# Reordering the two kinds of step in a convolution and soft-mixture kernel: the order of an odd and an even step's parts

## The chip, the cores and the metric

The kernel runs on one core of a Trainium2 chip. The time is device time in microseconds (us) of one execution, from several executions of the same program; the median is quoted. One execution was also taken by the hardware profiler, and everything said of the inside of the kernel comes from that one.

Names used below: PE is TensorE (matrix products and transposes, results in PSUM banks), DVE is VectorE, ACT is ScalarE, POOL is GpSimd, SP is the sync engine, whose queue here issues nearly all transfers (DMAs). Each engine and the SP queue work through their own instructions strictly in the order of the program; they wait for each other by semaphores.

## The reference: what is computed

Two parts, one after the other, in float32:

```python
# x: (8, 5696, 128), h: (5696, 128)
Xf = np.fft.rfft(x, n=2*S, axis=1); Hf = np.fft.rfft(h, n=2*S, axis=0)
y  = np.fft.irfft(Xf * Hf[None], n=2*S, axis=1)[:, :S]     # long convolution
x  = y.reshape(45568, 128)
logits = x @ phi                                           # phi: (128, 32)
d = softmax of logits over the 45568 tokens                # column-wise
slot_in = d.T @ x                                          # 32 slots x 128
slot_out = relu(slot_in[e] @ w1[e]) @ w2[e]                # 8 experts, 4 slots each
c = softmax of logits over the 32 slots                    # row-wise
out = c @ slot_out                                         # (45568, 128)
```

## The kernel before: tiles, stages and the order of the work

The convolution is done as a two-level transform. A sequence of 5696 rows is seen as 89 by 64; the first level works along the 89, the second along the 64, and then the same way back. Between levels the data change their layout by going through DRAM: tensor `f` between the first and the second level, tensor `z` between the second level and the way back. The filter `h` goes through the first two levels as batch 0, the eight batches of `x` follow.

The main loop (line 583) runs over steps t = 0, 1, 2 ... 92. Nine batches of 8 chunks make 72 chunks, and step t < 72 takes chunk t. The pieces of work, each named by one letter in the dictionary `work_` (lines 607 to 628):

- `x`, `load_x` (L184, L195): two SP transfers, 320 KB and 36 KB, of chunk t+3 into one of three tiles `xc`.
- `f`, `fold` (L201, L206): two POOL additions (sum and difference of the chunk with its mirror image) of chunk t+1 into `xf`, four tiles, two for even and two for odd chunks.
- `X`, `first_low` (L217, L220, L226): first-level products of chunk t for 60 of the 90 frequencies, in 128x64 shape; two ACT evictions, two SP stores to `f` of 240 KB.
- `Y`, `first_high`: the remaining 30 frequencies of chunks t-1 and t together, on odd t only, in 128x32 shape; two evictions, four stores of 120 KB. It is the last reader of chunk t-1's folded tiles, which `f` of the same step overwrites.
- `p`, `P`, `prefetch` (L253): SP loads of second-level units `gt` from `f` (512 KB each, the last of a batch 128 KB). A batch has 12 units; odd steps work on one, even steps on two.
- `b`, `slot_b`: for a unit u, `stage_b1` (PE L267 in 64x64 shape, then four DVE instructions, L285 twice and L294 twice), and `stage_b2` of the unit before it (PE L309, also 64x64; two ACT evictions L315; one 512 KB store to `z`, L318).
- `z`, `load_pair` (L338, L346): SP loads of one pair of output columns from `z`: five transfers (1024 KB, three of 128 KB, 32 KB) into `zc`, of which there is one tile only.
- `1`, `stage_c1` (L365, L370, L371, L374, L378): the way back. Two products of `zc` (call them c1a), an eviction and two DVE additions; then the function `between`, which is `stage_c4` of an older pair (PE transposes L431, ACT, DVE L446, POOL L439 and L447); then two more products (c1b) and an eviction.
- `w`: the rest of `stage_c1`, two DVE additions and four POOL ones (L384).
- `2`, `stage_c2` (L393): sixteen transposes of the result, four evictions L395. `3`, `stage_c3` (L402): products with phi, the logits, evicted to `lt` by L405. `m`, `column_max` (L413 and on): running column maximum of `lt` on DVE. `5`, `stage_c5` (L454). `s`, `softmax` (L462 to L468). `6`, `stage_c6` (L504, store L515). `d`, `dispatch` (L480, L485): accumulation of `d.T @ x`.

Products of PE go through a ring of four PSUM banks; each new result waits until the one four before it has been read. The order of the letters is written out by hand, one string for odd and one for even t:

```python
ORDER_E, ORDER_O, XAHEAD = "xXYf1wb5s", "zPxXfb26db3m", 3
for c_ in (ORDER_E if t % 2 else ORDER_O):
    work_[c_]()
```

`ORDER_E` is used on odd t, `ORDER_O` on even t. An odd step and the even step after it are called a pair of steps here; a pair handles one `zc`. Pairs of the way back begin at t = 27 (lag `LAG_C`), second-level units at t = 9. The last chunk is t = 71, so from then on `x`, `X`, `Y` and `f` do nothing. After the loop comes a tail written out separately (lines 658 to 851) with the last pairs, the experts and the output.

Of the kernel before, what the change touches and what calls it, by code (L numbers as in the profile page):

```python
# [12 lines left out]
AL = mybir.AluOpType  # L13
# [64 lines left out]
def kernel(  # L78
# [24 lines left out]
    nc = tc.nc  # L103
# [3 lines left out]
    E, _, F = moe_w1.shape  # L107
# [12 lines left out]
    NQ = NJ // 2  # L120
# [57 lines left out]
    xs = {}  # L178
# [17 lines left out]
                out=t_[X0 + r.start:X0 + r.stop, :, :, :].rearrange("p s n d -> p s (n d)"), in_=v)  # L196
        xs[c] = t_

    folded = {}

    def fold(c, comp):  # L201
        if c not in xs:
            return
        t_ = xs.pop(c) if comp else xs[c]
        y_ = xf[c % 2 * 2 + comp]
        nc.gpsimd.tensor_tensor(out=y_[:, :, :], in0=t_[:, 0, :, :], in1=t_[:, 1, ::-1, :],  # L206
                                op=AL.subtract if comp else AL.add)
        folded[(c, comp)] = y_

    def first_stage(tiles, width):  # L210

        st = apool.tile([P, CH, 2, D], F32, name="fst", tag="fst", bufs=4)
        for G in range(2):
            p = bank()
            for o, (c, comp) in enumerate(tiles):
                k = slice(0, HP) if width == HP else slice(HP, HP + QP)
                nc.tensor.matmul(p[o * width:(o + 1) * width, :], s1[:, comp + G, k],  # L217
                                 folded[(c, comp)][:, :, :].rearrange("p n d -> p (n d)"),
                                 start=True, stop=True)
            nc.scalar.activation(st[:, :, G, :],  # L220
                                 p[:, :].rearrange("p (n d) -> p n d", d=D), AF.Copy)
        for o, (c, comp) in enumerate(tiles):
            g, j = divmod(c, NJ)
            n0 = comp * HALF + CH * j
            k0, n = (0, N1A) if width == HP else (N1A, N1 - N1A)
            nc.sync.dma_start(  # L226
                out=fd[g].rearrange("q a r c d -> (q a) (r c d)")[k0:k0 + n, n0 * 2 * D:(n0 + CH) * 2 * D],
                in_=st[o * width:o * width + n, :, :, :].rearrange("k n c d -> k (n c d)"))
# [2 lines left out]
        first_stage([(c, comp) for comp in range(2)], HP)  # L231

    def first_high(c):

        both = [(c - 1 + i, comp) for i in range(2) for comp in range(2)]
        first_stage(both, QP)
        for b_ in both:
            del folded[b_]

    gs, prods = {}, {}  # L240

# [107 lines left out]
                                    a=2)[r:r + n, j * w_:(j + 1) * w_])  # L349
        zs[T] = t_  # L350

    def stage_c1(T, between):
        t_ = zs.pop(T)
        kr = used if t_ is zn else P
        y_ = ybufs.pop(0)
        ybufs.append(y_)

        def part(v, f):
            k = (2 * v + f) * CH
            return y_[:, k:k + CH, 0:D] if f == 0 else y_[:, k + CH - 1:k - 1:-1, 0:D]  # L360

        def product(o, tab, q):
            p = bank()
            for h_ in range(2):
                nc.tensor.matmul(p[h_ * HP:(h_ + 1) * HP, :], i1[0:kr, tab, :],  # L365
                                 t_[0:kr, h_, o, :, q, :], start=True, stop=True)
            return p[:, :].rearrange("p (n d) -> p n d", d=D)

        def fold_out(even, minus, plus):
            nc.vector.tensor_tensor(out=plus, in0=even, in1=minus, op=AL.add)  # L370
            nc.vector.tensor_tensor(out=minus, in0=even, in1=minus, op=AL.subtract)  # L371

        b_, a_ = product(0, 1, 1), product(0, 0, 0)
        nc.scalar.activation(part(0, 0), b_, AF.Copy)  # L374
        fold_out(a_, part(0, 0), part(1, 0))
        between()
        b_, a_ = product(1, 1, 0), product(1, 2, 1)
        nc.scalar.activation(om[:, :, :], b_, AF.Copy)  # L378

        def after():  # L380
            fold_out(a_, om[:, :, :], op[:, :, :])
            for v, o_, eng in ((1, op, nc.gpsimd), (0, om, nc.vector if tail else nc.gpsimd)):
                for part_, sign in ((part(v, 1), AL.subtract), (part(v, 0), AL.add)):
                    eng.tensor_tensor(out=part_, in0=part(v, 0), in1=o_[:, :, :], op=sign)  # L384

        ys[T] = y_
        return after

    def stage_c2(T):
        for k in (3, 1, 0, 2) if tail else (3, 2, 1, 0):  # L390
# [187 lines left out]
    for comp in range(2):  # L578
        fold(0, comp)
    wait_b2 = []  # L580
    ORDER_E, ORDER_O, XAHEAD = "xXYf1wb5s", "zPxXfb26db3m", 3

    for t in range(last_front + 1):
        us = list(units(t))

        def pair(lag):
            T, half = divmod(t - LAG_C - lag, 2)
            return T if half == 0 and 0 <= T < NT else None

        def prefetch(last):  # L590
            nonlocal loaded
            while loaded < len(queue) and queue[loaded][1] <= last:
                load_g(queue[loaded][0])
                loaded += 1

        def slot_b():
            fresh = bool(us)
            if fresh:
                u = us.pop(0)
                stage_b1(u, t < LAG_C or t >= NA)  # L600
                wait_b2.append(u)
            if len(wait_b2) > fresh:
                stage_b2(wait_b2.pop(0))

        T, U = pair(0), pair(2)
        after = []
        work_ = {
            "z": lambda: load_pair(pair(-1)) if pair(-1) is not None else None,
            "x": lambda: load_x(t + XAHEAD) if t < NA else None,
            "p": lambda: prefetch(t + 1) if t % NJ else None,  # L610
            "P": lambda: prefetch(t + 2),
            "q": lambda: prefetch(t + 1),
            "X": lambda: first_low(t) if t < NA else None,
            "Y": lambda: first_high(t) if t < NA and t % 2 else None,
            "f": lambda: [fold(t + 1, comp) for comp in range(2)] if t < NA else None,
            "d": lambda: dispatch(pair(3)) if pair(3) is not None else None,
            "b": lambda: slot_b(),
            "1": lambda: after.append(stage_c1(T, lambda: stage_c4(U) if U is not None else None))
            if T is not None else stage_c4(U) if U is not None else None,
            "w": lambda: [a_() for a_ in after],  # L620
            "2": lambda: stage_c2(pair(1)) if pair(1) is not None else None,
            "6": lambda: stage_c6(pair(5)) if pair(5) is not None else None,
            "5": lambda: stage_c5(U) if U is not None else None,
            "3": lambda: stage_c3(pair(1)) if pair(1) is not None else None,
            "m": lambda: column_max(pair(1)) if pair(1) is not None else None,
            "s": lambda: list(softmax(U)) if U is not None else None,
            "g": lambda: prefetch(t + 1) if t % NJ == 0 else None,
        }
        if t == last_front:
            if pair(-1) is not None:  # L630
                load_pair(pair(-1))
            assert T is None and U is None
            if pair(3) is not None:
                dispatch(pair(3))
            slot_b()
            slot_b()
            slot_b()
            stage_c2(pair(1))
            slot_b()
            assert not us and not wait_b2  # L640
            V = pair(1)
            stage_c6(V - 2)
            stage_c3(V)
            column_max(V)
            break
        for c_ in (ORDER_E if t % 2 else ORDER_O):
            work_[c_]()
        assert not us
        if t == NA:
            lead.close()  # L650
            wts = inner.enter_context(tc.tile_pool(name="wts", bufs=1, side="right"))
            w1s = wts.tile([P, E, F], F32, name="w1s")
        if NA < t <= NA + E:
            nc.sync.dma_start(out=w1s[:, t - NA - 1, :], in_=moe_w1[t - NA - 1])
# [21 lines left out]
    tail["pool"] = cload.enter_context(tc.tile_pool(name="cload", bufs=2))  # L676
    y_ = tail["pool"].tile([P, Q * CH, D + 1], F32, name="y2", tag="y2", bufs=1)

    after = stage_c1(T, lambda: stage_c4(V))
    after()  # L680
    stage_c5(V)
    list(softmax(V))
    nc.gpsimd.memset(y_[:, :, D:D + 1], 1.0)
# [21 lines left out]
    for V in range(T, NT):  # L705
# [10 lines left out]
        N = T + 1 if V == T else V + 2  # L716
        after = None
        if N < NT:
            after = stage_c1(N, lambda: stage_c4(V))
            load_pair(N + 2)  # L720
        else:
            stage_c4(V)
        if after:
            after()
        if V > T:
            placed_c()
        stage_c5(V)
# [8 lines left out]
            list(end)  # L736
        if V == T:
            ybufs.insert(0, y_)
            stage_c1(T + 2, lambda: None)()
            load_pair(T + 4)  # L740
        else:
            for i in range(4 * (V - T - 1), min(4 * (V - T), E), 2):
                nc.sync.dma_start(
                    out=w2s[:, i:i + 2, :, :],
                    in_=moe_w2[i:i + 2].rearrange("e (p c) d -> p e c d", p=P))
    stage_c6(NT - 2)
    assert list(Ls) == [NT - 1] and not (ys or ds or prods or gs or zs or xs or folded or wait_b2
                or kept or landed)


# [129 lines left out]
```

## Time and profile before

| what | value |
|---|---|
| median of 3 runs | 869.77 us (869.0 to 874.97) |
| the profiled execution: its own time | 869.39 us |
| its span, first to last instruction | 867.6 us |
| granted TensorE clock, mean | 0.947 |
| PE busy | 774.3 us (89%) |
| DVE busy | 619.5 us (71%) |
| ACT busy | 442.6 us (51%) |
| POOL busy | 404.3 us (47%) |
| transfers | 272.46 MB, mean 314 GB/s, 90.2% of the 16 DMA engines' span on SP's queue |

The shares are averages over stages of a different kind. In time the stages are, by the trace: up to about 53 us the first level alone (chunks of `h` and the first of `x`); to about 99 us second-level units of `h`; to 177 us second-level units of `x` as well; from the first c1a at 176.96 us to 627.33 us the full pairs, 22 of them; to about 720 us pairs without first-level work; then the tail.

### The profile page before, as it was taken

The numbers are of one execution on the slowest core, as the hardware profiler recorded it, in microseconds if no ns is written. First come the engines' busy times: TensorE is split into PE (matmuls) and PEld (weight loads), VectorE is DVE, ScalarE is ACT, GpSimd is POOL, SyncE is SP. The second block draws the span as 40 slices with busy tenths as digits, with TensorE's granted clock in tenths as the row PEclk, the third lists the DMA queues.
The fourth block names the chain that finished last, engine by engine and source line by source line (L and its number), as shares of the span: only waits on it lengthen the run. The fifth ranks groups of instructions, "written<-read, shape, count | busy, mean of one in ns | idle before, by whom it ended". The sixth has DMA issues, their size and how long they took to land.

```text
span 867.6 us, 20501 instructions
## 1 busy us (share of the span) xinstructions
PE 774.3 (89%) x7796; PEld 380.7 (44%) x7796; DVE 619.5 (71%) x929; ACT 442.6 (51%) x906; POOL 404.3 (47%) x386
## 2 busy tenths in 40 slices
PE   5889788889999999999999999999998888968993
PEld 1223333234444444444444444444454444444882
DVE  3049867667778778877888788777788895963642
ACT  2433244435555555655565565555544444773541
POOL 4453424245565566656566555555434332671000
PEclk9999999999999999999999999999999898988855
DMA  9899999999999999999999999999997886670898
GB/s 294 258 300 316 299 326 351 324 327 332 341 326 342 334 329 334 337 330 338 339 348 337 335 328 338 337 326 335 316 330 276 286 308 252 245 305 2 338 405 337
DMA packets 156124, 272.46 MB, mean 314 GB/s; under 512 B 12198, under 2 KB 113702, under 8 KB 152885
## 3 DMA queue, kind: packets, MB, share of 16 engines
q1 hardware_dynamic: 155451, 270.85, 90.2%
q8 instruction: 62, 1.02, 0.5%
q10 hardware_dynamic: 576, 0.31, 0.1%
q14 instruction: 35, 0.29, 0.1%
HBM read 142.81 MB, written 128.21 MB: 312 GB/s over the span
## 4 chain that ended last, share of the span: by engine, by line
PE 55%; DMA 20%; DVE 11%; SPq 2%; issue 2%; POOL 1%; ACT 1%; DVEq 0%; ACTq 0%
PE bank L365 13%; PE bank L217 11%; DMA zc<-z 8%; PE bank L309 7%; PE bt L267 7%; PE bank L393 6%; DMA out_dram<-o 4%; DMA xc<-in_x_dram 4%; DMA gt<-f 3%; DVE yf L294 3%; PE bank L480 3%; DVE p L285 2%; DVE bt L285 2%; SPq L346 2%; PE bank L431 2%
## 5 line engine op out<-in xcount | busy, mean ns | idle before, releaser
L206 POOL TENSOR_TENSOR x<-xc 128x512 f32<-128x512 f32 x144 | 180.1, 1275 | 228.5 <-PE bank L217 196.4
L217 PE MATMUL bank<-x,s 128*32 128x512 f32 (+1 forms) x1152 | 227.4, 613 | 16.3 <-POOL x L206 15.4
L315 ACT ACTIVATE zst<-bank 128x512 f32<-128x512 f32 (+1 forms) x184 | 98.7, 586 | 190.5 <-PE bank L309 168.8
L220 ACT ACTIVATE fst<-bank 128x512 f32<-128x512 f32 x216 | 127.5, 598 | 109.5 <-PE bank L217 85.0
L285 DVE TENSOR_TENSOR p<-bt,Hi 128x1024 f32<-128x1024 f32 x96 | 111.3, 1160 | 34.0 <-PE bt L267 33.1
L365 PE MATMUL bank<-zc,i 128*64 128x512 f32 x480 | 117.5, 611 | 10.8 <-DMA f<-fst 6.4
L309 PE MATMUL bank<-yf,vt 64*64 64x256 f32 x1440 | 102.4, 390 | 26.8 <-DVE yf L294 26.8
L217 PEld LDWEIGHTS bank<-x,s 128*32 128x32 f32 (+1 forms) x1152 | 57.0, 124 | 154.3 <-issue 76.1
L294 DVE TENSOR_TENSOR yf<-bt,p 128x512 f32<-128x512 f32 x192 | 119.3, 662 | 3.3
L267 PE MATMUL bt<-gt,wt 64*64 64x256 f32 x1620 | 113.7, 388 | 6.0 <-DMA gt<-f 3.9
L285 DVE TENSOR_TENSOR bt<-bt,Hr 128x1024 f32<-128x1024 f32 x96 | 112.9, 1177 | 0.0
L267 PEld LDWEIGHTS bt<-gt,wt 64*64 64x64 f32 x1620 | 54.0, 132 | 80.9 <-issue 38.0
L384 POOL TENSOR_TENSOR y<-y,op 128x512 f32<-128x512 f32 x64 | 77.5, 1211 | 11.4 <-DVE op L370 8.3
L309 PEld LDWEIGHTS bank<-yf,vt 64*64 64x64 f32 x1440 | 57.0, 135 | 58.0 <-issue 27.8
L370 DVE TENSOR_TENSOR y<-bank,y 128x512 f32<-128x512 f32 x32 | 22.1, 691 | 70.9 <-PE bank L365 70.6
L393 PE MATMUL bank<-ident,y 109*128 109x109 f32 x512 | 66.1, 283 | 0.7 <-DVE y L384 0.7
L384 POOL TENSOR_TENSOR y<-y,om 128x512 f32<-128x512 f32 x54 | 64.1, 1186 | 2.1
L365 PEld LDWEIGHTS bank<-zc,i 128*64 128x64 f32 x480 | 31.2, 137 | 74.6 <-issue 45.9
L393 PEld LDWEIGHTS bank<-ident,y 109*128 109x128 f32 x512 | 55.9, 154 | 16.5 <-issue 11.1
L395 ACT ACTIVATE yt<-bank 128x360 f32<-128x360 f32 x128 | 51.7, 489 | 4.2 <-PE bank L393 4.2
L833 PE MATMUL op<-so,cT 32*128 32x128 f32 x704 | 45.8, 378 | 3.6 <-ACT o L842 2.9
L285 DVE TENSOR_TENSOR p<-bt,turn 128x1024 f32<-128x1024 f32 (+1 forms) x12 | 14.2, 1179 | 46.6 <-PE bt L267 45.7
(97 smaller groups left out, 817.3 us busy)
## 6 DMA issues: line engine op xcount, KB each, us to landing
gt<-f SPq DMA_DIRECT2D x99, 512.0 KB
z<-zst SPq DMA_DIRECT2D x88, 512.0 KB
f<-fst SPq DMA_DIRECT2D x144, 240.0 KB
zc<-z SPq DMA_DIRECT2D x30, 1024.0 KB
xc<-in_x_dram SPq DMA_DIRECT2D x64, 320.0 KB
f<-fst SPq DMA_DIRECT2D x144, 120.0 KB
out_dram<-o SPq DMA_DIRECT2D x16, 1024.0 KB
zc<-z SPq DMA_DIRECT2D x90, 128.0 KB
```

The source lines that it names most:

```text
L206: nc.gpsimd.tensor_tensor(out=y_[:, :, :], in0=t_[:, 0, :, :], in1=t_[:, 1, ::-1, :], op=AL.subtract if comp else AL.add)
L217: nc.tensor.matmul(p[o * width:(o + 1) * width, :], s1[:, comp + G, k], folded[(c, comp)][:, :, :].rearrange("p n d -> p (n d)"), start=Tr ...
L220: nc.scalar.activation(st[:, :, G, :], p[:, :].rearrange("p (n d) -> p n d", d=D), AF.Copy)
L267: nc.tensor.matmul(bt[q * HP:(q + 1) * HP, a, o, :], wt[r, 2 * i + q, :], t_[r, 2 * o + q, :, :].rearrange("p c d -> p (c d)"), start=True ...
L285: nc.vector.tensor_tensor(out=p_, in0=pv, in1=h_, op=AL.mult)
L294: eng.tensor_tensor(out=y_[r, 0:k, c, :], in0=pv[:, :, c, :], in1=pi[r, 0:k, 1 - c, :], op=op_)
L309: nc.tensor.matmul(bz[q][a * HP:(a + 1) * HP, o * 2 * D:(o + 1) * 2 * D], vt[r, i, a, :], y_[r, a * m + o, :, :].rearrange("p c d -> p (c ...
L315: nc.scalar.activation(st[:, 0:m, q, :], bz[q][:, 0:m * 2 * D].rearrange("p (o x) -> p o x", o=m), AF.Copy)
L365: nc.tensor.matmul(p[h_ * HP:(h_ + 1) * HP, :], i1[0:kr, tab, :], t_[0:kr, h_, o, :, q, :], start=True, stop=True)
L384: eng.tensor_tensor(out=part_, in0=part(v, 0), in1=o_[:, :, :], op=sign)
L393: nc.tensor.transpose(p[:, i * TR:(i + 1) * TR], ys[T][0:TR, k * CH + i, 0:D], ident[0:TR, 0:TR])
L395: nc.scalar.activation(yt[:, k * CH:(k + 1) * CH, :, :], of_tokens(p), AF.Copy)
```

## The change

Only the order changes; every instruction stays. `stage_c1` becomes a generator with two stopping points, so that `stage_c4` is no longer called from inside it but stands in the string as a letter of its own, `4`, and the second half of `stage_c1` as `j`. A letter `Z` loads the pair of the next odd step at the end of this odd step; it leaves out the first pair of a batch (`V_ % NQ == 0`), which `z` loads at the start of the even step as before. `folded` becomes a function in place of a dictionary, with the same tiles. In the tail the generator is stepped so that the order is what it was.

```diff
-    ORDER_E, ORDER_O, XAHEAD = "xXYf1wb5s", "zPxXfb26db3m", 3
+    ORDER_E, ORDER_O, XAHEAD = "Yf14jXwb5sZx", "zPxXfb26d3mb", 3
...
-    def stage_c1(T, between):
+    def stage_c1(T):
...
         fold_out(a_, part(0, 0), part(1, 0))
-        between()
+        yield
         b_, a_ = product(1, 1, 0), product(1, 2, 1)
         nc.scalar.activation(om[:, :, :], b_, AF.Copy)
...
         ys[T] = y_
-        return after
+        yield
+        after()
+        yield
...
+        def early(V_):
+            if V_ is not None and V_ % NQ:
+                load_pair(V_)
+
+        c1 = stage_c1(T) if T is not None else iter(())
         work_ = {
-            "z": lambda: load_pair(pair(-1)) if pair(-1) is not None else None,
+            "z": lambda: load_pair(pair(-1)) if pair(-1) is not None and pair(-1) not in zs else None,
+            "Z": lambda: early(pair(-2)),
...
-            "1": lambda: after.append(stage_c1(T, lambda: stage_c4(U) if U is not None else None))
-            if T is not None else stage_c4(U) if U is not None else None,
-            "w": lambda: [a_() for a_ in after],
+            "1": lambda: next(c1, None),
+            "4": lambda: stage_c4(U) if U is not None else None,
+            "j": lambda: next(c1, None),
+            "w": lambda: next(c1, None),
...
-    after = stage_c1(T, lambda: stage_c4(V))
-    after()
+    after = stage_c1(T)
+    next(after)
+    stage_c4(V)
+    next(after)
+    next(after)
```

In an odd step the new order is: Y, fold, c1a, c4, c1b, X, the rest of c1, the unit, c5, softmax, the loads of `zc`, the load of x. Before it was: load of x, X, Y, fold, c1a, c4, c1b, the rest of c1, the unit, c5, softmax, and the loads of `zc` at the start of the next step. In an even step the second unit and the pair logits, column maximum change places: dispatch, logits, column maximum, second unit.

## The prediction

> **What bounds the kernel now.** I read the engines' busy time by stage first, since an average over the span mixes stages. The windows' columns are: length, busy us of PE, PE weight loads, DVE, ACT and POOL with instruction counts, granted PE clock, share of the 16 DMA engines, GB/s.
>
> ```profile
> 8.00:53.00 45.00, 37.69 (x168) 10.57 (x172) 1.40 (x5) 17.43 (x30) 23.87 (x21) 1.00 0.90 294
> 53.80:98.80 45.00, 38.75 (x292) 13.55 (x292) 42.20 (x48) 14.33 (x24) 19.68 (x17) 1.00 0.93 308
> 98.80:177.00 78.20, 62.52 (x602) 24.82 (x603) 53.15 (x60) 32.18 (x57) 26.87 (x22) 0.96 0.98 330
> 177.00:627.30 450.30, 441.30 (x4496) 204.27 (x4497) 355.88 (x544) 260.77 (x537) 256.81 (x237) 1.00 0.97 334
> 627.30:720.00 92.70, 77.98 (x840) 44.09 (x840) 79.41 (x121) 42.12 (x89) 34.31 (x35) 0.89 0.87 299
> ```
>
> Stage A (to 53) has no full engine. B (to 99) is DVE's: 42.2 of 45.0. C (to 177) is the transfers': 0.98. D (to 627), half of the time, has two: PE busy 98%, transfers 0.97. E (to 720) leans on DVE.
>
> Next the chain of waits (start, us, what) over a pair of D.
>
> ```profile
> 418.72 3.72 PE bank L217 x24
> 422.44 1.87 PE bank L365 x8
> ...
> 426.76 1.02 PE bt L267 x16
> 427.79 0.86 PE bank L309 x16
> ...
> 438.97 3.72 PE bank L217 x24
> ...
> 455.99 6.44 DMA zc<-z
> ...
> 462.95 1.94 PE bank L365 x8
> ```
>
> From 418.72 to 438.97 it is PE without a gap: 20.25 us a pair (19.88 where the small unit falls). Yet every few pairs it leaves PE for the `zc` load. L267 and L309 move the same amount (16 passes of 256 columns, 64x64); L267, which follows another shape, takes 1.02, L309 directly after it 0.86. A change of shape costs 0.16.
>
> Then the waits in 265 to 640 (in total, times, longest), PE's and the SP queue's.
>
> ```profile
> PE bank L365 <- DMA zc<-z: 3.5, 5, 1.3
> PE bank L309 <- DVE yf L294: 3.2, 5, 1.8
> ```
>
> ```profile
> SPq L195 <- DMA zc<-z: 23.3, 20, 2.7
> SPq L318 <- DMA gt<-f: 20.3, 16, 2.2
> SPq L318 <- ACT zst L315: 1.4, 5, 0.4
> ```
>
> SP waits for landings, hardly ever for an eviction. The semaphores in the trace say why: SP's transfers use eight in turn, so each waits until the one eight places earlier has landed. SP issues stores 6 to 9 us after their data are ready. In D the stream of transfers runs by itself, 20.47 us a pair (c1a at 176.96 and 627.33, 22 pairs), and PE, with 20.16 on average, meets it at `zc`: the last piece lands between 1.3 us before PE is free and 1.3 after. Both are the bound, evenly.
>
> Last, stage A's timeline.
>
> ```profile
> 26.20 4.93 POOL L206 TENSOR_TENSOR x<-xc 128x512 f32<-128x512 f32 x4 [3.96 <-PE bank L217]
> 27.51 3.52 PE L217 MATMUL bank<-x,s 128*64 128x512 f32 x10 [1.43 <-POOL x L206]
> 31.18 3.79 PE L217 MATMUL bank<-x,s 128*64 128x512 f32 x22 [0.15 <-POOL x L206]
> 35.08 4.94 POOL L206 TENSOR_TENSOR x<-xc 128x512 f32<-128x512 f32 x4 [3.96 <-PE bank L217]
> ```
>
> POOL does four folds, waits 3.96 for X and Y of the odd step, folds again: 8.89 a pair, POOL and PE taking turns.
>
> **The change part by part.** The sum is against the profiled execution, 869.39 us (span 867.6 and 1.79 around it), 0.38 below the median of the three runs.
>
> *Y ahead of X, stage A.* The fold waits for Y, the last reader of the old tiles. With Y first, X (half of 3.79, 1.9) runs beside the fold: 8.89 becomes 7.0. Against it, the x load of an odd step moves behind that step's six stores (3.8 us of issue): issued 4.6 us after Y's end and landing 3.7 later, at 8.3, where the fold that wants it could start at 7.0. Fold and Y from there, 4.95 + 1.7, close two pairs in 14.95: 7.5 each. Four pairs save 5.6. But the first `gt` load reads what X of step 7 stores, and X comes after Y now. Followed step by step: Y of step 7 ends at 37.2 (before 43.9), X is evicted at 39.8, its stores stand behind Y's four and land at 44.2, `gt` lands 4.4 later, L267 takes 1.1: DVE's first unit starts near 49.9 in place of 53.84. I take -3.9; ends 0 and -7.6 (4 x 1.9).
>
> *Stage B.* DVE's work cannot shrink; its waits for `gt` can (PE waits 2.6 for it, DVE idles 2.8 of 45). The `gt` load no longer depends on the x load's landing eight places before, but on a store's. -1; ends 0 and -2.8.
>
> *Stage C* is the transfers'; the same bytes: 0. Ends: -3.3 (PE's idle time before the first c1a) and +1.9 (X no longer fills it).
>
> *Stage D, PE.* X after c1b is the same 128x64 shape; logits after dispatch the same 128x32: of thirteen changes of shape a pair (X, Y, c1a, c4, c1b, unit, c5, X, unit, c2, dispatch, unit, logits, and round again) eleven are left, -0.32 us. c1b ends 1.87 earlier in the step, so DVE's chain op, om, p, yf in front of L309 gains room (3.2 us of waits).
>
> *Stage D, transfers.* Bytes and number (24 a pair) stay. Adding up the seven transfers that may still be under way when one is issued: before, least at the odd unit's z store, 996 KB, and the DMA share falls there (0.78 in 269 to 271); in the new order the least is 1284 KB. The store waits less and the queue runs dry less. I expect the stream to gain 0.2 us of the 0.6 that a share of 1.00 would give. 22 x 0.2 = -4.4. Ends: -14.1 (PE alone, 19.83 on average, -0.64 each) and +18.9 (every pair like the slow one from 278.88 to 300.21, 21.33).
>
> *What the moved loads pass.* `zc`'s load only passes from the start of the even step to the end of the odd one: neighbours on SP. What leaves its front is the x load, 356 KB, some 1.0 us of the stream; this now stands between `zc` and `gt`, whose first load had 2.9 us to spare (landed 280.28, used 283.20). x of an odd step lands 1 us after `zc`; its fold needs it at Y's end, about c1a's start. Queued behind the fold on POOL are L439, L447 and four L384: 2.5 + 0.1 + 1.05 + 4.9 = 8.6 us, and the transposes L393 need the last of them 13.7 us after c1a's start. So x may land 5.1 after it: cover of 4 us; beyond that every microsecond costs one per pair. X's two stores are ready 6.8 us after c1a's start, SP reaches them at 8.1; the z store 9.0 and 9.9. Zero, with 0.9 us of cover.
>
> *Column maximum ahead of the second unit.* DVE now waits for the logits' eviction, then 1.4 us of maximum, then the unit. In D the next c1a leaves room (its sum is wanted 6.95 after dispatch, DVE is free at 6.7). In E there is no X and Y: the chain there goes through DVE. Before, after dispatch (660.3) the unit starts at 661.37 and the maximum ends at 666.41; after, logits end at 660.9, eviction at 661.7, maximum at 663.3, unit at 667.0. +0.6, four pairs: +2.4; ends -0.6 (0.16 of PE each) and +6 (the whole maximum).
>
> The tail keeps its order: 0. Sum: 869.4 - 3.9 - 1 - 4.4 + 2.4 = **862.5 us**.
>
> The Trainium skill's Perfetto Trace Analysis (Roofline) gives about 435 GB/s as the ceiling of the 16 engines; by it the row of 334 GB/s has room, PE would be D's only bound, and the sum would be 852.8. The row beside it is the share of 0.97 and SP waiting for landings, so I don't go by it. DMA: Bandwidth & Descriptors (Why a DMA increments its semaphore by 16 and not by 1) speaks against the change: a transfer uses only as many engines, the lowest ones, as divide its outer count, so pieces of 8 rows use eight and stores of 60 or 30 rows fifteen; by that the fullest engines carry 463 KB a pair where the mean is 416, the stream has no room whatever the mean share says, and the sum would be 866.9. No row here shows single engines.
>
> **The rivals.**
> 1. *PE decides D.* For it: PE runs without a gap over whole pairs; against: SP never waits for evictions. -14.1 in place of -4.4: 852.8 us.
> 2. *The stream decides D and order is nothing to it.* For it: 0.97 to 1.00 share; against: the dips. 869.4 - 4.9 + 2.4 = 866.9 us. PE's idle time would grow to 0.6 a pair, at `zc`.
> 3. *The stream gets slower*, loads now standing together (zc, x, gt, x) with no stores between. Point: above 20.58 a pair it ends slower than before. If x goes at gt's rate (about 300 GB/s, 1.2 us in place of 1.0 for 356 KB): +0.2, 871.3; at the end of the range, 21.33, 885.8. For it: 128 KB pieces of `zc` land 0.6 us apart; against: nothing waits longer in FIFO order by bytes.
>
> **How the numbers follow.** My forecast 0.45, with a range of its own of 857 to 868; rival 1 0.20, rival 2 0.25, rival 3 0.10. A measurement of this kernel can tell about 1%, 8.7 us, from no change: faster is below 861.1. Of my own case about 0.4 lies there, 0.18, and rival 1: 0.38. Slower than 878.5 is most of rival 3's upper part and things I haven't seen: 0.08. The rest 0.54. The range from rival 1 to a little beyond the smaller price of rival 3: 851 to 872.
>
> **What would show it.** Stage A: POOL's wait before four folds 2.1 to 2.6, not 3.96; first L285 near 50. D: L217 after L365 1.71, L402 0.6; the distance of c1a's 20.2 to 20.3 with PE waiting at `zc` in most pairs (rival 1: 19.9 and no wait; rival 2: 20.4). E: L413 before the unit's L285 and DVE's idle time in front of it. I am wrong if SP waits for ACT in D, if POOL's fold waits for x by more than 5 us, or if D's pairs exceed 20.47.

## The result, and the profile after

The changed kernel takes 901.07 us (median of four runs, 892.3 to 907.14), the kernel before 869.78 beside it: a ratio of 1.031, 95% interval 1.022 to 1.041. The ratios, here and in the experiments, and the medians in the table of the experiments leave out runs more than 1.5% above the fastest of the same kernel (here 907.14). Over the other three the median is 898.7 us, slower by 29 us; the forecast was 862.5, its range 851 to 872. The profiled execution is the fastest of the four, 892.3 us (span 890.5), so the trace shows 22.9 of the 29 us. They lie here (the bounds are starts of c1a, L360 in the new numbering, L365 before; all differences in us):

| stretch | before | after | difference | forecast |
|---|---|---|---|---|
| start to the first c1a (stages A to C) | 176.96 | 181.22 | +4.3 | -4.9 |
| 22 full pairs (D) | 450.37 | 469.25 | +18.9 | -4.4 |
| five pairs without first-level work (E) | 97.69 | 94.67 | -3.0 | +2.4 |
| the rest | 142.58 | 145.36 | +2.8 | 0 |

A pair of D takes 21.33 us in place of 20.47. The stages of the kernel after, in the columns of the table before:

```profile
8.00:53.00 45.00, 41.20 (x178) 10.06 (x180) 1.72 (x6) 17.92 (x30) 25.79 (x21) 0.96 0.89 293
53.00:99.00 46.00, 37.53 (x286) 12.31 (x284) 39.02 (x43) 12.60 (x22) 17.47 (x14) 0.96 0.92 292
99.00:181.20 82.20, 59.41 (x600) 23.84 (x599) 56.05 (x66) 32.65 (x58) 27.48 (x22) 0.93 0.97 323
181.20:650.50 469.30, 439.64 (x4498) 209.76 (x4499) 358.21 (x543) 263.36 (x537) 256.56 (x237) 0.98 0.99 320
650.50:745.00 94.50, 78.63 (x876) 44.33 (x876) 80.26 (x123) 45.35 (x96) 34.65 (x36) 0.95 0.89 302
```

The fourth line is the one to read. PE is as busy as before (440 us in place of 441) in a longer stage. The transfers' share rose from 0.97 to 0.99 and their rate fell from 334 to 320 GB/s. A busy share near 1 is therefore no measure of a rate: the same bytes kept the engines busy for longer. PE's and POOL's waits in D say where that arrives:

```profile
POOL x L206 <- DMA xc<-in_x_dram: 85.5, 13, 8.5
...
PE bank L360 <- DMA zc<-z: 24.9, 14, 3.1
```

Before, in the same stage, POOL's fold never waited for x, and PE waited for `zc` like this:

```profile
PE bank L365 <- DMA zc<-z: 3.0, 4, 1.3
```

So PE waits 24.9 us for `zc` in place of 3.0, and POOL's fold up to 8.5 us for x. And the SP queue after:

```profile
SPq L248 <- DMA zc<-z: 40.8, 24, 3.8
...
SPq L195 <- DMA zc<-z: 14.1, 23, 1.4
...
SPq L313 <- ACT zst L310: 4.9, 5, 1.3
```

SP still hardly waits for an eviction. A new line stands at the top: the `gt` load (L248) waits for `zc`. The queue's own timeline of one pair shows it (start, us, transfers at the end of the line), after and then before:

```profile
296.80 3.52 SPq L341 DMA_DIRECT2D zc<-z  x5
300.42 0.76 SPq L195 DMA_DIRECT2D xc<-in_x_dram  x2
301.23 5.57 SPq L248 DMA_DIRECT2D gt<-f  x3
306.89 0.80 SPq L195 DMA_DIRECT2D xc<-in_x_dram  x2
```

```profile
311.04 3.67 SPq L346 DMA_DIRECT2D zc<-z  x5
314.76 1.93 SPq L253 DMA_DIRECT2D gt<-f  x3
317.87 1.17 SPq L195 DMA_DIRECT2D xc<-in_x_dram  x2
```

Three `gt` take 5.57 us to issue in place of 1.93: each transfer waits for the one eight places earlier. Counted from `zc`'s 1024 KB, the ninth waits for it. Before, that was the x load. Now the two x transfers stand in between, and it is the second `gt`.

Following the landings, the 0.86 us a pair are about 0.5 at `zc` (from the landing ahead of it to its last piece 5.81 us on average, 5.35 before) and about 0.5 at the two 320 KB x transfers (1.06 us each after the landing ahead, 0.81 before; right behind `zc` 1.41), less 0.15 at `gt`. Stores cost what they did.

### The profile page after: what moved, and what is told of

It is laid out like the page before. It is cut to its first block, busy times and chain, and to the rows that moved or that the text cites. A ratio compares the mean times of both kernels' runs of the same rounds, so it can differ in the third digit from the quotient of the medians.

```text
span 890.5 us, 20402 instructions
## 1 busy us (share of the span) xinstructions
PE 771.6 (87%) x7796; PEld 382.6 (43%) x7796; DVE 622.9 (70%) x929; ACT 444.0 (50%) x906; POOL 404.1 (45%) x386
## 4 chain that ended last, share of the span: by engine, by line
PE 47%; DMA 32%; DVE 10%; SPq 4%; issue 3%; ACT 2%; POOL 1%; DVEq 0%; ACTq 0%; POOLq 0%
PE bank L216 13%; DMA zc<-z 11%; PE bank L360 10%; DMA gt<-f 6%; PE bt L262 6%; DMA z<-zst 5%; PE bank L304 4%; DMA out_dram<-o 4%; PE bank L390 4%; SPq L341 3%; DVE yf L289 2%; DVE p L280 2%; DVE bt L280 2%; PE bank L477 2%; PE bank L428 2%
## 5 line engine op out<-in xcount | busy, mean ns | idle before, releaser
L360 PE MATMUL bank<-zc,i 128*64 128x512 f32 x480 | 122.1, 632 | 36.5 <-DMA zc<-z 24.9
L304 PEld LDWEIGHTS bank<-yf,vt 64*64 64x64 f32 x1440 | 57.8, 134 | 54.9 <-issue 24.9
L360 PEld LDWEIGHTS bank<-zc,i 128*64 128x64 f32 x480 | 32.2, 141 | 101.1 <-issue 76.9
L390 PE MATMUL bank<-ident,y 109*128 109x109 f32 x512 | 63.8, 275 | 0.7 <-DVE y L379 0.7
L390 PEld LDWEIGHTS bank<-ident,y 109*128 109x128 f32 x512 | 53.3, 149 | 16.4 <-issue 10.1
L465 POOL TENSOR_TENSOR L<-L,rs 128x512 f32<-128x512 f32 x32 | 33.6, 1050 | 55.6 <-DVE rs L464 37.4
L365 DVE TENSOR_TENSOR y<-bank,y 128x512 f32<-128x512 f32 x32 | 22.1, 690 | 51.9 <-PE bank L360 51.5
L410 DVE TENSOR_REDUCE mx<-lt 64x1 f32<-64x360 f32 x64 | 33.1, 518 | 31.6 <-ACT lt L402 31.1
```

Source lines behind the costliest of these rows:

```text
L304: nc.tensor.matmul(bz[q][a * HP:(a + 1) * HP, o * 2 * D:(o + 1) * 2 * D], vt[r, i, a, :], y_[r, a * m + o, :, :].rearrange("p c d -> p (c ...
L390: nc.tensor.transpose(p[:, i * TR:(i + 1) * TR], ys[T][0:TR, k * CH + i, 0:D], ident[0:TR, 0:TR])
```

## The experiments

The old order in the new letters is `"xXYf14jwb5s"`, `"zPxXfb26db3m"`; "odd" and "even" below are the two strings, and where only one is named the other is that of the order it starts from. Time per pair is the mean distance over D's 22 pairs of c1a starts in the profile of that run; for `zc` in three in the new order none is given. The letters K, M, L and O, later W and S, stand for theories; each is explained in the expectation that first uses it.

| run | median us | ratio to before (95%) | us a pair |
|---|---|---|---|
| before | 869.8 to 872.4 | 1 | 20.47 |
| the change | 898.7 | 1.031 (1.022 to 1.041) | 21.33 |
| x first | 886.4 | 1.015 (1.011 to 1.019) | 20.92 |
| only x and zc late | 903.1 | 1.035 (1.031 to 1.039) | 22.09 |
| two tiny transfers | 887.5 | 1.018 (1.012 to 1.023) | 21.10 |
| x ahead of zc | 892.6 | 1.023 (1.019 to 1.028) | 21.45 |
| even step only | 872.8 | 1.003 (0.999 to 1.006) | 20.42 |
| odd step's products only | 883.0 | 1.015 (1.010 to 1.019) | 21.04 |
| zc behind c1b, new order | 883.8 | 1.016 (1.010 to 1.021) | 20.90 |
| zc behind c1b, old order | 872.8 | 1.003 (1.000 to 1.007) | 20.61 |
| less PE: old order | 870.4 | 1.000 (0.996 to 1.005) | 20.47 |
| less PE: new order | 900.7 | 1.035 (1.033 to 1.037) | 21.61 |
| less PE: odd products | 883.1 | 1.015 (1.013 to 1.017) | 21.03 |
| zc behind X | 880.5 | 1.011 (1.008 to 1.013) | 20.62 |
| x behind gt | 905.8 | 1.040 (1.032 to 1.048) | 21.63 |
| zc in three, new order | 963.1 | 1.104 (1.097 to 1.111) | |
| zc in three, old order | 948.9 | 1.085 (1.078 to 1.093) | 22.69 |
| Y ahead of X only | 881.3 | 1.013 (1.008 to 1.018) | 21.04 |
| x between stores | 866.8 | 0.996 (0.993 to 0.999) | 20.45 |
| four load groups | 886.0 | 1.018 (1.014 to 1.023) | 20.73 |

### First four: the x load's place

```diff
-odd "Yf14jXwb5sZx"
+odd "xYf14jXwb5sZ"
```

> The new order, only the odd step's x load put back at that step's start (xYf14jXwb5sZ); all else as in the changed kernel. Theories: K (credits): the two x transfers between zc and gt use up two of the eight places, so that the second gt must wait for zc's 1024 KB; M (mix): a load standing directly behind zc's pieces lands slowly (x 1.41 us behind zc, 0.89 behind a z store), whatever the places; L (late x): POOL's fold waits for an x that lands too late (85 us of waits in the new order) and passes it on; O (order of products): Y, c1, X in the new order, or zc asked for 1.87 us earlier in the step, cost it. K, M and L: the pair's distance goes back to 20.3 to 20.5 us (after 21.33, before 20.47) and the time to 862 to 872. O: distance stays near 21.3, time 885 to 902.

886.4 us, 20.92 a pair. x's place is worth some 12 us (14 by the ratios), about half of the loss. No theory said so: K, M and L gave all of it, and of O's forecast the time (885 to 902) just holds the result, the distance (21.3) does not.

```diff
-odd "xXYf14jwb5s"
+odd "XYf14jwb5sZx"
```

> The kernel before, with only the odd step's two loads moved: zc and then x at the odd step's end (XYf14jwb5sZx); X, Y, c1 and the even step as before. K, M and L: nearly the whole loss without the rest of the change: distance 21.1 to 21.4, time 883 to 902. O: as before, 20.5, 867 to 873.

903.1 us, 22.09 a pair: the late loads alone cost as much as the whole change, more than K, M and L gave, and O falls. With the run before this one it means that the parts do not add up: they overlap.

```diff
+idle = [const.tile([1, NSL], F32, name=f"idle{i}") for i in range(2)]
...
+"t": lambda: [nc.sync.dma_start(out=i_[:, :], in_=moe_phi[0:1, :]) for i_ in idle] if LAG_C - 1 <= t < NA else None,
...
-even "zPxXfb26db3m"
+even "ztPxXfb26db3m"
```

> The kernel before, with two additional transfers of 128 bytes each between zc's last piece and the first gt, in steps 26 to 70; everything else as before. They carry nothing, but they take two of the eight places, as x does in the new order. K: the second gt waits for zc's 1024 KB (SP blocked 2 to 4 us there), distance 20.9 to 21.4, time 879 to 891. M, L and O: nothing is late and nothing is moved, distance 20.5 to 20.6, 868 to 873.

887.5 us, 21.10 a pair: 15 us for 256 bytes a pair. Its SP waits and its D as one window:

```profile
SPq L249 <- DMA zc<-z: 41.9, 33, 2.7
```

```profile
177.10:641.40 464.30, 442.70 (x4496) 204.73 (x4497) 355.84 (x544) 260.88 (x537) 256.44 (x237) 0.99 0.95 324
```

The `gt` load waits for `zc` as in the new order (41.9 and 40.8 us), and here the share falls to 0.95: the stream runs dry. The tiny transfers' own landings take 0.1 of the 0.63 us a pair. K's ranges hold: that a place costs time when what stands behind it is late is shown.

```diff
-odd "Yf14jXwb5sZx"
+odd "Yf14jXwb5sxZ"
```

> The new order with x and zc exchanged at the odd step's end (x, then zc, then gt). x is still late by most of a step, but zc and the three gt stand together again, and x stands behind the z store. K and M: distance 20.3 to 20.6, 862 to 874. L: x lands a few us earlier than in the new order, so some of the loss is left, 20.8 to 21.2, 875 to 895. O: 21.3, 885 to 902.

892.6 us, 21.45: K and M both said 20.3 to 20.6. Here `gt` keeps its places and the stream is slow all the same. K alone fails, and M in my wording ("directly behind zc") too; L's range held the time, not the distance, and O's forecast (21.3, 885 to 902) comes near in both, though the late loads alone had cost the whole loss without O.

### Next four: what the rest of the change costs

```diff
-even "zPxXfb26db3m"
+even "zPxXfb26d3mb"
```

> The kernel before with only the even step's letters exchanged (d3mb in place of db3m). With x back at its old place the new order was still 1.5% slower than before (20.92 us a pair), so a second cause stands beside the x load's place. Theory W (window): X between c1b and the odd unit brings that unit's z store 1.7 us later after c1a (evicted at the earliest 9.1 us in place of 7.4), and zc behind it on SP, while the next c1a comes no later; SP can no longer run ahead, and every late landing reaches PE. Theory S (second unit last): the even step's second unit, behind logits and maximum, brings its z store later and SP waits for it. W: this run is like before, 20.3 to 20.5 us a pair, 866 to 873. S: most of the rest, 20.8 to 21.0, 878 to 888.

872.8 us: no difference that can be told. S falls.

```diff
-odd "xXYf14jwb5s"
+odd "xYf14jXwb5s"
```

> The kernel before with only the odd step's products exchanged (Y, fold, c1a, c4, c1b, X; the x load first as before, zc at the even step's start; the even step as before). W: the rest of the loss without the even step's part, 20.8 to 21.1 us a pair, 880 to 890. S: like before but for the first stages, 20.3 to 20.5, 868 to 875.

883.0 us, 21.04, as W gave: the exchange of the odd step's products costs 12 us by itself.

```diff
-odd "Yf14jXwb5sZx"
+odd "xYf14jZXwb5s"
```

> The new order with x back at the odd step's start and zc's load moved up to directly behind c1b, ahead of X's two stores and the unit's z store (xYf14jZXwb5s). zc then no longer waits for anything behind X. W: the window is wide again, PE does not idle at zc, the pair falls to 19.8 to 20.4, 857 to 872. S, or a stream that has its own pace whatever is shifted: no gain on the 20.92 of the run with zc behind the store, 880 to 890.

883.8 us; W gave 857 to 872. The pair that opens a batch took 22.5 to 24.6 us: its first `gt` waits for the landing of X's last stores, which now stand behind `zc`. The others ran at PE's pace, 19.4 to 19.9 us with PE idle for 0.2 us at most, or, three times right behind the slow one, 21.3 to 21.5 at a granted clock of 0.92 or 0.93 (the first, at the start of D, 21.1). Two pairs, one of each kind:

```profile
308.15:327.55 19.40, 19.40 (x205) 9.34 (x201) 16.36 (x26) 12.18 (x25) 11.91 (x11) 1.00 0.95 312
327.55:351.96 24.41, 19.82 (x205) 9.29 (x201) 17.60 (x28) 12.33 (x25) 14.38 (x13) 1.00 0.87 295
```

No run here keeps these pairs and mends the one that opens a batch at no other cost.

```diff
-odd "xXYf14jwb5s"
+odd "xXYf14jZwb5s"
```

> The kernel before with only zc's load moved up to directly behind c1b (xXYf14jZwb5s). W: zc issues up to 1.8 us earlier than behind the z store; PE's idle time at zc, 0.3 us a pair before, goes, and the pair falls to 20.2: 862 to 868. A stream with its own pace: 20.47, 868 to 873.

872.8 us, no gain: against W.

### Less work for PE: is PE a bound at all?

```diff
-            p = bank()
-            for o, (c, comp) in enumerate(tiles):
+            p = bank() if G == 0 or tiles[-1][0] < LAG_C else p
+            for o, (c, comp) in enumerate(tiles if G == 0 or tiles[-1][0] < LAG_C else []):
```

> The old order with half of the first level's products left out from step 27 on (the second of the two evictions reads the first product's bank again; sine parts are missing in the result, all transfers stay). PE's need falls by 2.9 us, to some 17.3 us a pair, so that the stream of transfers shows its own pace in this order. If PE was half of the bound (waits in both directions): 18 to 20.0 us a pair, 820 to 862. If the stream alone is the bound: 20.2 to 20.5, 864 to 870.

> The same half of the products left out in the new order. K (places): the stream's own pace is slower in this order, whatever PE does: 0.6 to 1.0 us a pair above the old order with the same products left out, 20.8 to 21.4, 880 to 893. Coupling only (PE and stream wait for each other, each fast enough by itself): the same distance as the old order, within 0.2.

> The same half of the products left out in the old order with only the odd step's products exchanged (slower by 1.5% with all products, 21.04 us a pair in its profile). W (window): its stream is as fast as the old one's by itself, and the loss was PE and stream waiting for each other: within 0.2 of the old order with the same products left out. If the order of the stores itself slows the stream: 0.4 or more above it.

870.4, 900.7 and 883.1 us: each order keeps its time. PE's work in like pairs at full clock fell by 2.5 us (20.33 to 17.85 in the old order), somewhat less than the 2.9 that I had counted. D of the three, in this order:

```profile
177.20:627.50 450.30, 395.21 (x4144) 188.68 (x4144) 372.15 (x540) 253.78 (x535) 256.76 (x238) 0.97 0.97 335
```

```profile
181.10:656.50 475.40, 401.03 (x4144) 194.97 (x4144) 358.05 (x544) 258.28 (x537) 256.95 (x237) 0.95 0.99 317
```

```profile
181.60:644.20 462.60, 396.77 (x4144) 194.66 (x4144) 365.91 (x544) 255.81 (x537) 256.37 (x237) 0.96 0.97 326
```

PE's busy time (the figure behind the length) falls by 39 to 46 us against the same order with all products; the length of the stage stays, or grows by 6 us (new order). The stream sets D in all three orders, and its pace depends on the order: 20.47, 21.61, 21.03. W falls with this: the loss is no waiting of PE and stream for each other.

```diff
-odd "Yf14jXwb5sZx"
+odd "xYf14jXZwb5s"
```

> The new order with x at the odd step's start and zc's load between X's stores and the unit's z store (xYf14jXZwb5s). Directly behind c1b it made three pairs of four run at PE's pace (19.4 to 19.8) and cost it again at each batch's first pair, where the first gt waited up to 5.8 us for X's stores to land behind zc. Here X's stores go first, and zc still does not wait for the unit behind X. W: 19.8 to 20.4 us a pair, 860 to 872. If the stream has its own pace in every order: 20.8 to 21, 880 to 888.

880.5 us: D is at 20.62, but five us were lost ahead of it and four behind, in E. W again gave less.

### The stream's order

```diff
+"v": lambda: load_x(t + 2) if 0 < t <= NA else None,
...
-odd "Yf14jXwb5sZx", even "zPxXfb26d3mb"
+odd "Yf14jXwb5sZ", even "zPvxXfb26d3mb"
```

> The new order with the odd step's x load not between zc and gt but behind gt, directly ahead of the even step's x load. zc and the three gt then have the eight places that they had before; zc, gt, x and x still stand together with no store between. K (places): back to the run with x at the step's start, 20.9 us a pair, 880 to 888. M (loads together): as slow as the new order, 21.2 to 21.5, 890 to 903.

905.8 us, 21.63 a pair, more than either theory gave; 14 us of it are lost ahead of the first c1a (191.1 us, before 177.0). `gt` no longer waits for `zc`; the x loads behind it do (before 27.0 us, 24 times):

```profile
SPq L195 <- DMA zc<-z: 39.8, 61, 2.5
```

So the order is slow with x behind `zc`, ahead of it and behind `gt`, but here not by x itself: its two 320 KB transfers land 0.89 and 0.79 us after the landing ahead, about as before. The time went into `gt` (5.55 us a pair, before 5.06) and `zc` (5.67, before 5.35). Of these places the odd step's start cost least, where x stands apart from the other loads, with stores on both sides. That this is the reason (M, widened) is a guess; the last two runs below test it.

```diff
-    left = [(64 + 8 * j, min(8, n - 64 - 8 * j), j, 4) for j in range((n - 57) // 8)]
-    return [(0, 64, 32, 1)] + left
+    return [(0, 64, 32, 1), (64, 16, 0, 1), (80, n - 80, 16, 1)]
...
-    held = slice(N1 // 64 * 8 + 3, used - 64, 4)
+    held = slice(N1 - 64, used - 64)
```

> The new order with zc in three transfers (64, 16 and 10 rows of 16 KB, to other partitions; the table of the products follows) in place of five, so that a pair has 22 transfers, and the second gt no longer waits for zc. The bytes are the same. K: at least the 14 us that x in front would bring, 20.3 to 20.9 us a pair, 870 to 888. M: 21.1 to 21.4, 890 to 902.

> The kernel before with zc in three transfers (64, 16 and 10 rows) in place of five; order of all letters as before. If the three transfers are slow by their layout (fewer engines or other partitions for the 26 last rows), this run loses as much as the new order did with them (64 us above the new order): 920 to 945. If the loss came from more load bytes outstanding together in the new order: 866 to 890.

963.1 and 948.9 us: both orders lose, 64 and 78 us, so the three transfers are slow in any order, and the test of K is spoilt. In the old order the 256 KB into 16 neighbouring partitions landed 1.54 us after the piece ahead; before, 128 KB into eight partitions, four apart, took 0.58. The 1024 KB ahead of them, whose layout is the same, also took longer (4.70 us in place of 3.32). That the layout of the small pieces is the whole reason is therefore not shown.

```diff
-odd "xXYf14jwb5s"
+odd "xYXf14jwb5s"
```

> The kernel before with Y ahead of X in the odd step and nothing else (xYXf14jwb5s): four stores of 120 KB stand ahead of the two of 240 KB, all products stay ahead of c1. If the exchange of the stores is what the exchange of products cost (12 us): 20.9 to 21.1 us a pair, 878 to 886. If it is X's place behind c1b (its stores and the z store ready 1.7 us later): 20.4 to 20.6, 868 to 874.

881.3 us, 21.04: no product has moved behind c1, only the four stores of 120 KB now stand ahead of the two of 240 KB, and that is about all that the exchange of the products cost (883.0).

```profile
180.00:643.00 463.00, 441.23 (x4498) 208.31 (x4498) 381.41 (x544) 260.49 (x536) 256.53 (x237) 0.99 0.97 325
```

PE and the share are as before, 325 GB/s in place of 334. Most of the difference lies in the loads behind the stores: `zc` takes 5.81 us in place of 5.35, the first `gt` 0.1 more (1.66, 1.57). Ahead of `zc` nothing differs: the store before it lands 3.3 or 3.4 us after `zc` is issued in both orders. Why the loads are slower stays open.

```diff
-odd "xXYf14jwb5s", even "zPxXfb26db3m"
+odd "XxYf14jwb5s", even "zPXxfb26db3m"
```

> The kernel before with each x load moved behind X, between stores (XxYf14jwb5s and zPXxfb26db3m): a pair's loads stand in three groups in place of two. M: the stream gains as much as it lost by one group, 0.3 to 0.5 us a pair, until PE's 20.16 holds it: 20.1 to 20.3, 860 to 867. K alone: 20.4 to 20.7, 868 to 876.

866.8 us, 4.5 us under the kernel before beside it (871.3): the interval just excludes 1, but the pair (20.45) gains less than M gave, and most of what the profile gains lies in E (94.9 us in place of 97.7), where this run's order is that of the kernel before. So it does not show that grouping helps.

```diff
-odd "xXYf14jwb5s", even "zPxXfb26db3m"
+odd "XxYf14jwb5s", even "zXPxfb26d3mb"
```

> The old order with both x loads between stores, gt behind X's two stores in the even step, and the even step's new end (XxYf14jwb5s and zXPxfb26d3mb). Loads then stand in four groups a pair: zc; gt and x; x; each with stores between. M: 19.9 to 20.3 us a pair, PE's need being 19.9 here, 856 to 866. K or no effect of groups: 20.4 to 20.7, 867 to 875.

886.0 us where M gave 856 to 866. X's two stores now stand between `zc` and `gt`, and the waits show what they took:

```profile
SPq L248 <- DMA zc<-z: 29.7, 29, 2.4
```

It is the tiny transfers' case again (K), with 0.26 us a pair, and 7 us more ahead of the first c1a. A count of load groups predicts nothing as long as places are lost, and M stays unshown.

## Why the prediction was wrong

**The step that failed is "Stage D, transfers"**: -4.4 us forecast, +18.9 measured. That this is exactly the upper end given there is chance, since that end took one slow pair's length for all. The time went beyond the end of rival 3 that rests on it (885.8; 0.10), because the stages ahead and the rest lost too; anything above 878.5 had been given 0.08. I added up the bytes under way at each issue and took the least of them (996 KB before, 1284 after) as the sign that the queue would run dry less. A number that the sum left out mattered: how many places lie between a long transfer and the next load. One more pair of transfers behind `zc` makes the second `gt` wait for it (40.8 us of SP's waits in D). The two tiny transfers show that cost alone (15 us).

"What the moved loads pass" put the same x load at nothing: it weighed its 1.0 us of the stream against 2.9 us of room at the first `gt`, and not its two places. With x back at the step's start some 12 us are saved. And the order of the stores had no term in D: Y's four ahead of X's two cost 10 us alone (21.04 us a pair in place of 20.47), for a reason that stays open.

I also wrote, against rival 3, that nothing waits longer in order by bytes; x took 1.41 us behind `zc` and 0.89 behind a store. That a lost place costs time is shown. That loads standing together are slower is not: with x ahead of `zc` or behind `gt` the kernel was 6 and 19 us above the run with x first though `gt` kept its places, but nothing singles out the reason. How the 29 us divide is not shown either, since the parts overlap.

**"Both are the bound, evenly" was wrong as well.** PE meeting the stream at `zc` within 1.3 us looked like two bounds; it was one, with PE's work just fitting in. With 2.5 us less of it nothing got faster. The changes of shape were saved as forecast (PE's work in a pair at full clock fell from 19.81 to 19.46 and from 20.33 to 19.91 us, where I had 0.32) and were worth nothing. In no run here was D as short as rival 1 (852.8) needs; single pairs were, at PE's pace, as with `zc` behind c1b.

My estimate by the Trainium skill's DMA: Bandwidth & Descriptors (Why a DMA increments its semaphore by 16 and not by 1), 463 KB a pair on the fullest engines where the mean is 416, left the stream no room whatever PE does; the runs with less PE work agree with that, though no run shows single engines. Of the order the count says nothing: with equal transfers and less PE work the orders differ by 1.1 us a pair (20.47 and 21.61).

**Stage A, -3.9.** The wait that took the place of the removed one is the x load, as I had named it, but later:

```profile
24.79 4.94 POOL L206 TENSOR_TENSOR x<-xc 128x512 f32<-128x512 f32 x4 [3.54 <-DMA xc<-in_h_dram]
32.47 4.94 POOL L206 TENSOR_TENSOR x<-xc 128x512 f32<-128x512 f32 x4 [2.74 <-DMA xc<-in_h_dram]
41.91 4.92 POOL L206 TENSOR_TENSOR x<-xc 128x512 f32<-128x512 f32 x4 [4.50 <-DMA xc<-in_x_dram]
```

The pairs take 7.68 and 9.44 us, not 7.5, and DVE's first unit starts at 52.68 (forecast 49.9, before 53.84). Then B and C lose 5.4 us (forecast -1 and 0) at 292 and 323 GB/s in place of 308 and 330. Y ahead of X alone brings the first c1a to 180.0 (before 177.0), so 3 of the 4.3 us come with it.

**Column maximum, +2.4.** Not shown either way. E is 3.0 us shorter in this profile, but between runs whose order in E is the same it differs by more: 94.0 to 98.6 us in seven profiles with the old order there, 94.7 to 101.6 in five with the new. The run with the even step alone has E 0.9 shorter and a time that can't be told from before.

**What held.** x was late for its fold (my mark was 5 us; it waited up to 8.5), SP hardly waited for ACT, and pairs above 20.47 were the sign that I named for being wrong. One reading was too narrow, and nothing in the sum rests on it: SP issued D's stores before 2 to 12 us after their data were ready, not 6 to 9.

## What to carry to other kernels

Where each transfer waits for the one n places earlier, count places, and not only bytes: a small transfer put behind a long one makes the load after it wait, and two of 128 bytes cost 15 us here. Places alone did not tell the order's time either, so try the order of stores and loads one exchange at a time. Before weighing two bounds against each other, take work from one of them; if the time stays, leave its terms out of the sum. A share of busy transfer engines near 1 can say that the stream is the bound, not how fast it is: read the GB/s beside it. And before a gain of a few us is put down to a change, compare stages that the change leaves alone: here one differed by 4 us and more between profiles.

## What the runs showed of the hardware

The second-level loads are slower than stores of their size: landing after landing, 512 KB of a `z` store took 1.32 us (397 GB/s), 512 KB of `gt` 1.82 (288), on average over D before. It is no rule for all loads: 320 KB of x took 0.81 us (about 400 GB/s). The reason for the difference was not tested.

PE's clock can fall after a wait, and the products behind it take longer. The chain after, around a c1a (at 264.76) in front of which PE idles 2.08 us for `zc`, and a window behind it with the granted clock (third figure from the end):

```profile
242.99 1.94 PE bank L360 x8
244.93 0.59 PE bank L428 x4
245.52 1.87 PE bank L360 x8
...
257.57 7.05 DMA zc<-z
...
264.76 2.56 PE bank L360 x8
267.32 1.05 PE bank L428 x4
268.37 2.37 PE bank L360 x8
```

```profile
265.94:269.35 3.41, 3.41 (x12) 1.16 (x10) 1.63 (x3) 1.48 (x3) 0.00 (x0) 0.50 1.09 326
```

The same sixteen products and four transposes take 5.98 us in place of 4.40, and the pair's granted clock is 0.92. The Trainium skill's TensorE: Matmul & The Clock Gate (Part 1) puts the fall to half rate behind an idle window of about 3.4 us that runs freely. Here shorter idle times were enough: in front of a c1a in D, 2.1 to 3.1 us were followed by the fall four times, and four others of 2.5 to 2.9 were not. That it cost D nothing, since the stream was late anyway, is likely but was not tested.

For `zc` in three pieces, the skill's SBUF — State Buffer (Door 1: The DMA port swizzle) has a rule that fits: four neighbouring partitions share a port, so 16 rows in a row reach four of sixteen, and eight rows four apart reach eight. The two runs agree in sign (64 and 78 us); no run here shows single ports, and the rule does not say why the unchanged 1024 KB took longer too.
